# Dense weights unpacked one chunk further ahead, and token sums that begin later

## The chip, the cores and the metric

The kernel runs on one core of a Trainium2 chip. The metric is the device time of one execution in microseconds. The kernel before takes 569.09 us (median of three runs, 568.45 to 571.18).

## The reference

Three stages follow each other on the same 1536 tokens. Only the last one is touched by the change.

```python
attn_out = _attn_ref(q, k, v, n_sink, window)          # 2 x 8 heads, 768 positions, 64 wide; window of 128 and 4 sinks
x = attn_out.transpose(0, 2, 1, 3).reshape(1536, 512)
x = _moe_ref(x, w_gate, w1, w2)                        # 8 experts, 192 tokens each: relu(x @ w1[e]) @ w2[e]

def _moe2_ref(x, w_in, w_out):                         # the dense stage
    h = x @ w_in                                       # 512 -> 2048
    g = h * (1.0 / (1.0 + np.exp(-h)))                 # silu
    return (g @ w_out).astype(np.float32)              # 2048 -> 512
```

`w_in` and `w_out` are drawn as float64, so each of their numbers comes as two 32-bit words. The experts' weights are float32.

## The kernel before, in words

**Numbers in two halves.** A product is made from numbers split in a high and a low half (`float32r`): high by high, high by low, low by high, all added in one PSUM bank. So a chunk of weights goes through these steps before TensorE can use it: two or more loads of 512 KB on SP's queue (`raw`, lines 888 to 893); for the float64 ones the unpacking of the two words into a float32 tile `f64`, ten VectorE steps a half chunk (`s0` to `s4` twice, lines 912 to 932); and the split, a copy on ScalarE (`hi`, line 955) and a subtraction (`lo`, line 958) that is GpSimd's for float32 chunks and VectorE's for the late float64 ones.

**Chunks.** The class `Weights` numbers the chunks: 0 to 31 are the experts', 32 and 33 the first input and output chunk of the dense stage, then for each of three further parts of 512 hidden columns two input chunks and one output chunk: 34, 35, 36, then 37, 38, 39, then 40, 41, 42. The output chunks 36, 39 and 42 have two halves, each with a `hi` and a `lo`. The input chunks 34, 35, 37, 38, 40 and 41 go through `mix` (line 980) instead: besides two blocks as they are, four sums and differences of their blocks are made on GpSimd and split, ten GpSimd instructions a chunk (lines 1004, 1008 and 1015). `early` are 32 and 33, unpacked during the attention; `late` are 34 to 42.

**Two queues of steps.** `split(k)` is called when a buffer of the four `wr` buffers is given back (`done`). It puts the unpacking of chunk k in line (`ahead`, list `back`) and its split in line (list `todo`). In `dense`, after each turn, `W.pump(1, 1)` issues one step of `todo`, if its chunk is unpacked, and one step of `back`. The order of the engines' instructions is thus written out when the program is built: every engine runs its own in this order, and an instruction that must wait holds up all that is behind it on its engine.

**Passes of `dense`.** The loop over `n` (line 1466) makes 17 passes. Pass n computes the hidden columns of slot n (part c of four, token group g of two, half p of the part's columns), and the output products (`down`, line 1384) of slot n - 1. Passes 0 to 5 are plain: four products `u` of 12 matmuls (line 1271, 384 columns) and six `d` turns of 6 matmuls (line 1393, 512 columns), in the order `uuddduuddd`; pass 0 has no `d`. From pass 6 (`MIX`) on, seven `u` of 6 matmuls and six `d` take turns; a product over sums of tokens and sums of weights replaces one in four there, and some products are added into a tile `keep` on VectorE (line 1305), which frees the bank. The product banks `h` are two. ScalarE makes `Silu` (1257) and the high half of the result (1258), VectorE its low half (1450, `gt`). In the second and third part, six output tiles of a group are added to running sums, loaded from and stored to HBM (lines 1374, 1405 and 1409); this is in passes 6, 8, 10 and 12, and in the last part the sum goes out by rows.

**Token sums.** The mixed form needs sums and differences of the tokens. `mixing` (line 1319) gives them as lists of steps, 20 for each group (`made`), most of them one VectorE instruction (line 1426), six a copy on ScalarE (1329) and a subtraction on VectorE (1330), and eight more a group that overwrite x in its place (`placed`). The list `extra` holds them with the pass and turn from which each may be issued, and `also` issues one, or two in certain passes, behind each turn:

```python
extra = deque([(0, 0, f) for f in made[0][0] + made[1][0]] + ...)
def also(n, k):
    for _ in range(2 if n in (0, begin - 1) else 1): ...
```

Of the kernel before, what the change touches and what calls it, by code (L numbers as in the profile page):

```python
# [871 lines left out]
class Weights:  # L872
# [64 lines left out]
    def split(self):  # L937
        nc, k = self.nc, self.ns
        if k >= len(self.order):
            return  # L940
        self.ns += 1
        w = self.pool.tile([P, 2, CH], F32R, name="wr", bufs=self.depth)
        wide = k in self.wide
        self.ahead(k)
        if k in self.mixed:
            self.todo += [(0, f, (k, 0)) for f in self.mix(k, w, wide)]
            return
        for half in range(2):
            sl = slice(half * CH // 2, (half + 1) * CH // 2)

            def src(half=half):
                return self.box[k, half][0].bitcast(F32) if wide else self.raw[k][0]

            def hi(sl=sl, src=src):
                nc.scalar.activation(w[:, 0, sl], src(), AF.Copy)  # L955

            def lo(half=half, sl=sl, src=src):
                (nc.vector if k in self.late else nc.gpsimd).tensor_tensor(  # L958
                    w[:, 1, sl], src(), w[:, 0, sl].bitcast(F32), OP.subtract)
                self.used(k, half, w)  # L960
            self.todo += [(0, hi, (k, half)), (0, lo, (k, half))]

    def fresh(self):
        while self.full >= self.scratch:
            self.todo.popleft()[1]()
        self.full += 1
        return self.f64.tile([P, CH // 2], I32, name="f64", bufs=self.scratch)
# [132 lines left out]
def ffn(tc, rows, idx, ident, W, out, sums_d, mix_d):  # L1100
    with ExitStack() as ctx:
        x2 = ctx.enter_context(tc.tile_pool(name="f_x", bufs=1, side="right")).tile([P, 4, 2, B * S], F32R, name="x2")
        kk = [0]

        def nxt():
            kk[0] += 1
            return kk[0] - 1

        with rows.ctx, tc.tile_pool(name="e_p", bufs=1, space=PSUM) as pp:
            experts(tc, rows, lambda name: pp.tile([P, 2, 512], F32, name=name, bufs=2), ident, W, nxt, x2)  # L1110
        with tc.tile_pool(name="d_w", bufs=1, reuse_waits="tile") as gp, \
                tc.tile_pool(name="d_p", bufs=1, space=PSUM, reuse_waits="tile") as pp:
            dense(tc, gp, pp, idx, W, nxt(), x2, out, sums_d, mix_d)
# [123 lines left out]
def dense(tc, wp, pp, idx, W, first, x2, out, sums_d, mix_d):  # L1237
# [81 lines left out]
    def mixing(g):  # L1319
        t, q = keep[:2]  # L1320

        def at(j, s, b, d):
            return x2[:, 2 * j + d, b, tokens(g, s)].bitcast(F32)

        def tt(*a):
            return partial(nc.vector.tensor_tensor, *a)

        def split(dst, src, after=lambda: None):
            nc.scalar.activation(dst[0], src, AF.Copy)
            nc.vector.tensor_tensor(dst[1], src, dst[0].bitcast(F32), OP.subtract)  # L1330
            after()

        def keep_it():
            for n in range(3):
                nc.sync.dma_start(mix_d[g, :, n], xn[:, n].rearrange("p a d t -> p (a d t)").bitcast(F32))

        def new(n, d):
            return [xn[:, n, b, d] for b in range(2)]

        made, placed = [], []  # L1340
        for d in range(2):
            made += [
                tt(t, at(0, 1, 0, d), at(0, 0, 0, d), OP.subtract),
                tt(q, at(0, 1, 1, d), at(0, 0, 1, d), OP.subtract),
                tt(t, t, q, OP.add),
                partial(split, new(0, d), t),
                tt(q, at(1, 1, 0, d), t, OP.subtract),
                tt(q, q, at(1, 1, 1, d), OP.add),
                partial(split, new(1, d), q),
                tt(t, at(1, 0, 0, d), q, OP.subtract),  # L1350
                tt(t, t, at(1, 0, 1, d), OP.add),
                partial(split, new(2, d), t, keep_it if d else lambda: None),
            ]
            placed += [
                tt(t, at(1, 1, 0, d), at(0, 1, 0, d), OP.subtract),
                tt(q, at(1, 1, 1, d), at(0, 1, 1, d), OP.subtract),
                tt(t, t, q, OP.add),
                partial(split, [x2[:, d, b, tokens(g, 1)] for b in range(2)], t),
            ]
        return made, placed  # L1360
# [23 lines left out]
    def down(c, g, p, t, ahead):  # L1384
# [18 lines left out]
        def add():  # L1403
# [6 lines left out]
            if ahead is not None:  # L1410
# [3 lines left out]
    slots = [(c, g, p) for c in range(4) for g in range(2) for p in range(2)]  # L1414
    begin = slots.index(MIX)
    made = [mixing(g) for g in range(2)]
    extra = deque([(0, 0, f) for f in made[0][0] + made[1][0]] + [(4, 0, f) for f in made[1][1]] +
                  [(begin - 1, 2, f) for f in made[0][1]])

    def halves(n):  # L1420
        return (0, 1) if n < begin - 1 else (1, 0)

    def also(n, k):
        for _ in range(2 if n in (0, begin - 1) else 1):
            if extra and extra[0][:2] <= (n, k):
                extra.popleft()[2]()  # L1426

    for n in range(len(slots) + 1):
# [14 lines left out]
        for k, turn in enumerate(turns):  # L1443
            src = u if turn == "u" else down_at
            if not src:
                continue
            due = len(later)
            src.pop(0)()
            for _ in range(due):
                later.popleft()()  # L1450
            W.pump(1, 1 if n else 0)
            also(n, k)
# [223 lines left out]
```

## Time and profile before

| | |
|---|---|
| median of three runs | 569.09 us |
| profiled execution | 571.69 us, span 569.8 us |
| mean granted TensorE clock | 0.988 |
| TensorE busy | 546.6 us (96%) |
| VectorE busy | 354.9 us (62%) |
| ScalarE busy | 292.5 us (51%) |
| GpSimd busy | 287.0 us (50%) |
| DMA | 107.90 MB, mean 189 GB/s |

The span runs from the first to the last instruction, and the profiled execution's time is 1.89 us more. A busy share is a mean over stages with different limits; `dense` begins near 292 us and takes the rest. In `dense` TensorE is the engine that the others must keep up with, so what counts there is when it had to wait and what it waited for. In the rows further down, "idle" or a bracket before an arrow gives how long an engine stood before the instruction, and behind the arrow stands what released it. Matmul ends are modelled, so waits of TensorE are better read from the starts of its instructions.

### The profile page before, as it was taken

Reading aid. Unit: us, or ns where it says so; the run is one execution under the profiler, and the core shown is the slowest. Engines: PE = TensorE matmul, PEld = TensorE weight load, DVE = VectorE, ACT = ScalarE, POOL = GpSimd, SP = SyncE. Lnnn points to the kernel's source line nnn. Section 1 sums busy time; section 2 is a strip of 40 time slices with the busy share of each in tenths; the row PEclk is TensorE's granted clock in tenths of the full one; section 3 lists DMA queues with packets and bytes.
Section 4 is the critical chain, followed back from the end, with each engine's and each line's share of the span. In section 5 each row is a group of like instructions: output and inputs, shape, how many; then the busy total and the mean of one; then the engine's idle time right before and its main releaser. Section 6 shows DMA issues by size and latency. Waiting matters only on the chain.

```text
span 569.8 us, 9684 instructions
## 1 busy us (share of the span) xinstructions
PE 546.6 (96%) x3389; PEld 481.7 (85%) x3389; DVE 354.9 (62%) x923; ACT 292.5 (51%) x576; POOL 287.0 (50%) x278
## 2 busy tenths in 40 slices
PE   8999999878999999999999999998999999989996
PEld 4678677756999999999998899886997898979984
DVE  3788998773543443434358797875878657795423
ACT  4545554754676776777634563641454334544330
POOL 4334343296699999999990254200354006420404
PEclk9999999899999999999999999998999899999999
DMA  7998752144566666667640551623767647347602
GB/s 203 357 381 273 264 172 94 57 159 158 166 198 230 221 223 226 222 219 225 216 132 15 213 197 73 223 94 126 223 224 238 236 173 255 123 162 245 234 18 110
DMA packets 43934, 107.90 MB, mean 189 GB/s; under 512 B 4650, under 2 KB 12458, under 8 KB 43884
## 3 DMA queue, kind: packets, MB, share of 16 engines
q1 hardware_dynamic: 41696, 100.88, 52.7%
q0 software_dynamic: 1920, 6.29, 3.1%
q8 instruction: 27, 0.44, 0.3%
q14 instruction: 23, 0.19, 0.1%
q10 hardware_dynamic: 268, 0.10, 0.1%
HBM read 86.81 MB, written 20.45 MB: 188 GB/s over the span
## 4 chain that ended last, share of the span: by engine, by line
PE 59%; DVE 5%; issue 5%; DMA 2%; ACT 2%; POOL 2%; POOLq 0%; SPq 0%; DVEq 0%; another core or an unknown queue 0%; ACTq 0%
PE acc L1393 17%; PE h L1271 16%; PE mm L1178 8%; PE m L1201 8%; PE mm L1181 4%; PE m L1204 4%; DMA os<-sums_d 2%; POOL out L1364 2%; PE mm L1201 1%; DVE keep L1426 1%; DVE wr L958 1%; ACT wr L955 1%; PE mm L1137 1%; DVE os L1405 1%; DMA row<-x_d,idx 1%
## 5 line engine op out<-in xcount | busy, mean ns | idle before, releaser
L958 POOL TENSOR_TENSOR wr<-raw,wr 128x1024 fp32r<-128x1024 f32 x64 | 150.7, 2390 | 9.1 <-ACT wr L955 9.0
L1393 PE MATMUL acc<-wr,gt 128*128 128x512 f32 x576 | 148.6, 400 | 6.1 <-DVE wr L958 3.0
L1393 PEld LDWEIGHTS acc<-wr,gt 128*128 128x128 f32 x576 | 108.1, 190 | 28.1 <-DVE wr L958 4.3
L1271 PE MATMUL h<-x,wr 128*128 128x384 f32 x528 | 101.5, 338 | 1.8 <-ACT keep L1257 1.4
L1271 PEld LDWEIGHTS h<-x,wr 128*128 128x128 f32 x528 | 93.7, 188 | 6.2 <-ACT keep L1257 1.7
L1004 POOL TENSOR_TENSOR wr<-f,wr 128x512 fp32r<-128x512 f32 x12 | 16.7, 1394 | 127.6 <-ACT wr L999 67.4
L1178 PE MATMUL mm<-xg,wr 128*128 128x384 f32 x248 | 72.4, 360 | 0.5 <-DVE xg L1152 0.3
L955 ACT ACTIVATE wr<-raw 128x1024 fp32r<-128x1024 f32 x64 | 66.6, 1052 | 2.2 <-DMA raw<-in_w 1.3
L1201 PE MATMUL m<-ht,wr 128*128 128x384 f32 x224 | 66.0, 361 | 0.0
L1181 PE MATMUL mm<-xg,wr 128*128 128x192 f32 x248 | 62.1, 250 | 0.0
L1204 PE MATMUL m<-ht,wr 128*128 128x192 f32 x224 | 56.1, 250 | 0.0
L1450 DVE TENSOR_TENSOR gt<-keep,gt 128x384 fp32r<-128x384 f32 x64 | 38.4, 599 | 23.3 <-ACT gt L1258 23.2
L283 ACT ACTIVATE A<-t,nm 128x132 f32<-128x132 f32 x96 | 36.1, 400 | 30.9 <-DVE nm L274 30.7
L1178 PEld LDWEIGHTS mm<-xg,wr 128*128 128x128 f32 x248 | 46.4, 187 | 1.2 <-DVE xg L1152 0.7
L1181 PEld LDWEIGHTS mm<-xg,wr 128*128 128x128 f32 x248 | 47.2, 190 | 0.0
L1159 DVE TENSOR_TENSOR mm<-mm,t 128x384 f32<-128x384 f32 x33 | 18.7, 567 | 45.1 <-ACT t L1158 45.1
L305 POOL TENSOR_SCALAR_AFFINE_SELECT atd<-at 128x512 f32<-128x512 f32 x24 | 16.4, 685 | 59.2 <-ACT at L303 47.8
L1204 PEld LDWEIGHTS m<-ht,wr 128*128 128x128 f32 x224 | 42.7, 190 | 0.0
L1201 PEld LDWEIGHTS m<-ht,wr 128*128 128x128 f32 x224 | 42.0, 187 | 0.0
L1257 ACT ACTIVATE keep<-keep 128x384 f32<-128x384 f32 x30 | 15.8, 526 | 50.2 <-DVE keep L1305 50.2
L1298 ACT ACTIVATE keep<-h 128x384 f32<-128x384 f32 x30 | 14.7, 489 | 45.9 <-PE h L1271 42.0
L1271 PE MATMUL h<-xn,wr 128*128 128x384 f32 x180 | 38.2, 348 | 0.0
(197 smaller groups left out, 1012.9 us busy)
## 6 DMA issues: line engine op xcount, KB each, us to landing
raw<-in_w SPq DMA_DIRECT2D x64, 512.0 KB, 3.6
sums_d<-os SPq DMA_DIRECT2D x36, 256.0 KB, 2.1
xn<-mix_d SPq DMA_DIRECT2D x12, 768.0 KB, 5.2
raw<-in_wi SPq DMA_DIRECT2D x16, 512.0 KB, 4.4
raw<-in_wo SPq DMA_DIRECT2D x16, 512.0 KB, 4.3
os<-sums_d SPq DMA_DIRECT2D x24, 256.0 KB, 2.8
mix_d<-xn SPq DMA_DIRECT2D x6, 768.0 KB, 4.0
va<-in_va SPq DMA_DIRECT2D x12, 292.0 KB, 5.2
```

The source lines that it names most:

```text
L283: nc.scalar.activation(A[i][:, h], t, AF.Exp, bias=nm, scale=-1.0)
L955: nc.scalar.activation(w[:, 0, sl], src(), AF.Copy)
L958: (nc.vector if k in self.late else nc.gpsimd).tensor_tensor(w[:, 1, sl], src(), w[:, 0, sl].bitcast(F32), OP.subtract)
L1004: nc.gpsimd.tensor_tensor(w[:, 1, sl].rearrange("p (d f) -> p d f", d=4), src()[:, :, i * P:(i + 1) * P], w[:, 0, sl].bitcast(F32).rearran ...
L1159: nc.vector.tensor_tensor(h, h, t, OP.add)
L1178: nc.tensor.matmul(mm[:, b, :2 * CAP], w[:, 0, fb, d, o:o + P], x[:, d].rearrange("p a t -> p (a t)"), start=d == 0, stop=False, skip_grou ...
L1181: nc.tensor.matmul(mm[:, b, :CAP], w[:, 1, fb, d, o:o + P], x[:, d, 0], start=False, stop=d == 3, skip_group_check=True)
L1201: nc.tensor.matmul(mm[:, d % 2, :2 * CAP], w[:, 0, d // 2, f, o:o + P], ht[:, f].rearrange("p a t -> p (a t)"), start=c == 0 and f == 0, s ...
L1204: nc.tensor.matmul(mm[:, d % 2, :CAP], w[:, 1, d // 2, f, o:o + P], ht[:, f, 0], start=False, stop=last, skip_group_check=True)
L1271: nc.tensor.matmul(h, w(a, d), x(b, d), start=start and d == 0 and k == 0, stop=d == n - 1 and k == 2, skip_group_check=True)
L1393: nc.tensor.matmul(a, gt[:, u, ts], w[:, v, 2 * p + i], start=(p, i, k) == (0, 0, 0), stop=(p, i, k) == (1, 1, 2), skip_group_check=True)
L1450: later.popleft()()
```

## The change

It has three parts. `split(k)` also puts the unpacking of chunk k + 1 in line when both are late chunks. `fresh`, which issues steps of `todo` when all four `f64` tiles are taken, asserts that such a step is not still being unpacked; this adds no instruction. The first list of token sums begins at turn 2 of pass 0 instead of turn 0, that is with its third product, two steps a turn are issued in pass 1 alone (before: in passes 0 and 5), so that pass 0 has two of the steps (before: eight) and pass 1 twenty (before: ten).

```diff
--- before
+++ after
@@ -942,6 +942,8 @@
         w = self.pool.tile([P, 2, CH], F32R, name="wr", bufs=self.depth)
         wide = k in self.wide
         self.ahead(k)
+        if k in self.late and k + 1 in self.late:
+            self.ahead(k + 1)
         if k in self.mixed:
             self.todo += [(0, f, (k, 0)) for f in self.mix(k, w, wide)]
             return
@@ -962,6 +964,7 @@
 
     def fresh(self):
         while self.full >= self.scratch:
+            assert self.todo[0][2] not in self.unpacking
             self.todo.popleft()[1]()
         self.full += 1
         return self.f64.tile([P, CH // 2], I32, name="f64", bufs=self.scratch)
@@ -1414,14 +1417,14 @@
     slots = [(c, g, p) for c in range(4) for g in range(2) for p in range(2)]
     begin = slots.index(MIX)
     made = [mixing(g) for g in range(2)]
-    extra = deque([(0, 0, f) for f in made[0][0] + made[1][0]] + [(4, 0, f) for f in made[1][1]] +
+    extra = deque([(0, 2, f) for f in made[0][0] + made[1][0]] + [(4, 0, f) for f in made[1][1]] +
                   [(begin - 1, 2, f) for f in made[0][1]])
 
     def halves(n):
         return (0, 1) if n < begin - 1 else (1, 0)
 
     def also(n, k):
-        for _ in range(2 if n in (0, begin - 1) else 1):
+        for _ in range(2 if n == 1 else 1):
             if extra and extra[0][:2] <= (n, k):
                 extra.popleft()[2]()
 
```

The instructions of each engine stay the same in kind and number, TensorE's in order too. VectorE, ScalarE, GpSimd and SP get another order. Three places on VectorE follow; lines behind 943 are two or three higher after the change.

VectorE where `dense` begins, that is pass 0 and the first turns of pass 1, before (`keep_4671` and `keep_4672` hold token sums, `keep_4673` and `keep_4674` results of `Silu`, `x_2933` is x):

```order
L1426 TENSOR_TENSOR keep_4671<-x_2933 128x384
L1426 TENSOR_TENSOR keep_4672<-x_2933 128x384
L1450 TENSOR_TENSOR gt<-keep_4673,gt 128x384
L1426 TENSOR_TENSOR keep_4671<-keep_4671,keep_4672 128x384
L1330 TENSOR_TENSOR xn<-keep_4671,xn 128x384
L1450 TENSOR_TENSOR gt<-keep_4674,gt 128x384
L1426 TENSOR_TENSOR keep_4672<-x_2933,keep_4671 128x384
L1426 TENSOR_TENSOR keep_4672<-keep_4672,x_2933 128x384
L1450 TENSOR_TENSOR gt<-keep_4673,gt 128x384
```

and with the change:

```order
L1453 TENSOR_TENSOR gt<-keep_4673,gt 128x384
L1453 TENSOR_TENSOR gt<-keep_4674,gt 128x384
L1429 TENSOR_TENSOR keep_4671<-x_2933 128x384
L1453 TENSOR_TENSOR gt<-keep_4673,gt 128x384
L1429 TENSOR_TENSOR keep_4672<-x_2933 128x384
L1453 TENSOR_TENSOR gt<-keep_4674,gt 128x384
L914 TENSOR_SCALAR f_4762<-raw 128x512
L1429 TENSOR_TENSOR keep_4671<-keep_4671,keep_4672 128x384
L1333 TENSOR_TENSOR xn<-keep_4671,xn 128x384
L1453 TENSOR_TENSOR gt<-keep_4673,gt 128x384
```

The low halves `gt` of the first two products come first, then two subtractions for token sums, each behind a product; the first step with ScalarE (`xn`) comes behind the first unpacking step, which is pass 1's.

VectorE around the low half of the second half of chunk 36 (`f_5368` before, `f_5229` after), with the first running sum of pass 6 (`os`), before:

```order
L922 TENSOR_SCALAR f_5368<-f_5368 128x512
L926 SCALAR_TENSOR_TENSOR f_5368<-raw,f_5368 128x512
L930 SCALAR_TENSOR_TENSOR f_5368<-raw,f_5368 128x512
L914 TENSOR_SCALAR f_5502<-raw 128x512
L958 TENSOR_TENSOR wr<-f_5368,wr 128x1024
L918 TENSOR_SCALAR f_5502<-f_5502 128x512
L1405 TENSOR_TENSOR os<-acc,os 128x512
```

and with the change, where the first running sum of pass 6 comes 23 rows behind the low half:

```order
L930 SCALAR_TENSOR_TENSOR f_5229<-raw,f_5229 128x512
L914 TENSOR_SCALAR f_5385<-raw 128x512
L1453 TENSOR_TENSOR gt<-keep_4673,gt 128x384
L960 TENSOR_TENSOR wr<-f_5229,wr 128x1024
L918 TENSOR_SCALAR f_5385<-f_5385 128x512
L1453 TENSOR_TENSOR gt<-keep_4674,gt 128x384
L922 TENSOR_SCALAR f_5385<-f_5385 128x512
```

The low half stood among the first unpacking steps of pass 6 and now stands between two results of pass 5, with the unpacking of chunk 37 (`f_5385`) behind it.

VectorE in the second half of pass 8 (running sums `os`; additions into `keep`, line 1305 before and 1308 after; `f_5786` before and `f_5669` after are the first half of chunk 39, `f_5906` and `f_5779` its second half, `f_5890` chunk 40), before:

```order
L1450 TENSOR_TENSOR gt<-keep_4672,gt 128x384
L922 TENSOR_SCALAR f_5786<-f_5786 128x512
L1305 TENSOR_TENSOR keep_4673<-h,keep_4673 128x384
L1405 TENSOR_TENSOR os<-acc,os 128x512
L926 SCALAR_TENSOR_TENSOR f_5786<-raw,f_5786 128x512
L1450 TENSOR_TENSOR gt<-keep_4673,gt 128x384
L930 SCALAR_TENSOR_TENSOR f_5786<-raw,f_5786 128x512
L1305 TENSOR_TENSOR keep_4671<-h,keep_4671 128x384
L1405 TENSOR_TENSOR os<-acc,os 128x512
L914 TENSOR_SCALAR f_5906<-raw 128x512
L1450 TENSOR_TENSOR gt<-keep_4671,gt 128x384
L958 TENSOR_TENSOR wr<-f_5786,wr 128x1024
```

and with the change:

```order
L1308 TENSOR_TENSOR keep_4672<-h,keep_4672 128x384
L1408 TENSOR_TENSOR os<-acc,os 128x512
L930 SCALAR_TENSOR_TENSOR f_5779<-raw,f_5779 128x512
L1453 TENSOR_TENSOR gt<-keep_4672,gt 128x384
L914 TENSOR_SCALAR f_5890<-raw 128x512
L1308 TENSOR_TENSOR keep_4673<-h,keep_4673 128x384
L1408 TENSOR_TENSOR os<-acc,os 128x512
L960 TENSOR_TENSOR wr<-f_5779,wr 128x1024
L918 TENSOR_SCALAR f_5890<-f_5890 128x512
L1453 TENSOR_TENSOR gt<-keep_4673,gt 128x384
L922 TENSOR_SCALAR f_5890<-f_5890 128x512
L1308 TENSOR_TENSOR keep_4671<-h,keep_4671 128x384
L1408 TENSOR_TENSOR os<-acc,os 128x512
```

Before, the low half of chunk 39's first half stands last, behind the third addition into `keep`. Now that one stands ahead of the pass's first running sum, and the low half of the second half stands ahead of the third addition.

## Rows read from the trace of the kernel before

**Rows 1.** The page: busy time by engine, and TensorE's granted clock in 40 slices.

```profile
PE 546.6 (96%) x3389; PEld 481.7 (85%) x3389; DVE 354.9 (62%) x923; ACT 292.5 (51%) x576; POOL 287.0 (50%) x278
...
PEclk9999999899999999999999999998999899999999
```

**Rows 2.** Who TensorE waited for: us in total, times, longest.

```profile
PE acc L1393 <- DVE wr L958: 3.0, 4, 0.8
PE acc L1393 <- ACT wr L955: 3.0, 3, 1.5
PE h L1271 <- ACT keep L1257: 1.4, 1, 1.4
```

**Rows 3.** Timeline of TensorE, first products of passes: start, us, instruction, idle before.

```profile
301.65 4.49 PE L1271 MATMUL h<-x,wr 128*128 128x384 f32 x24 [1.36 <-ACT keep L1257]
...
318.59 4.39 PE L1271 MATMUL h<-x,wr 128*128 128x384 f32 x24
...
369.15 4.39 PE L1271 MATMUL h<-x,wr 128*128 128x384 f32 x24
...
387.27 1.22 PE L1271 MATMUL h<-x,wr 128*128 128x384 f32 x6
...
407.39 1.22 PE L1271 MATMUL h<-x,wr 128*128 128x384 f32 x6
...
423.14 1.22 PE L1271 MATMUL h<-x,wr 128*128 128x384 f32 x6
...
439.47 1.32 PE L1271 MATMUL h<-x,wr 128*128 128x384 f32 x6 [0.41 <-DVE keep L1305]
...
458.92 1.22 PE L1271 MATMUL h<-x,wr 128*128 128x384 f32 x6
...
474.67 1.31 PE L1271 MATMUL h<-x,wr 128*128 128x384 f32 x6
...
506.27 1.24 PE L1271 MATMUL h<-x,wr 128*128 128x384 f32 x6
...
524.09 1.22 PE L1271 MATMUL h<-x,wr 128*128 128x384 f32 x6
```

**Rows 4.** Stretches: PE, PEld, DVE, ACT, POOL busy (count), granted clock, DMA share, GB/s.

```profile
388.00:398.00 10.00, 7.71 (x29) 6.33 (x28) 4.54 (x8) 2.12 (x4) 0.00 (x0) 0.83 0.46 153
440.00:450.00 10.00, 8.49 (x33) 6.98 (x32) 7.06 (x14) 3.74 (x7) 0.00 (x0) 0.83 0.62 195
```

**Rows 5.** Timelines of GpSimd, VectorE and ScalarE around pass 0.

```profile
289.37 9.46 POOL L958 TENSOR_TENSOR wr<-f,wr 128x1024 fp32r<-128x1024 f32 x4
...
294.04 5.68 DVE L1426 TENSOR_TENSOR keep<-x 128x384 f32<-128x384 f32 x2
...
300.69 0.52 ACT L1329 ACTIVATE xn<-keep 128x384 fp32r<-128x384 f32 x1 [3.54 <-DVE keep L1426]
```

**Rows 6.** Timeline of VectorE, pass 8: a running sum, an unpacking step, an addition.

```profile
429.65 0.69 DVE L1405 TENSOR_TENSOR os<-acc,os 128x512 f32<-128x512 f32 x1 [1.32 <-DMA os<-sums_d]
430.26 0.42 DVE L922 TENSOR_SCALAR f<-f 128x512 int32<-128x512 int32 x1
...
438.87 0.55 DVE L1305 TENSOR_TENSOR keep<-h,keep 128x384 f32<-128x384 f32 x1
```

**Rows 7.** Unpacking: ten steps beside GpSimd (us, count), and a group alone (mean ns).

```profile
409.50:422.20 12.70, 8.96 (x10) 1.00 0.61 211
...
L926 DVE SCALAR_TENSOR_TENSOR f<-raw,f 128x512 int32<-128x512 int32 x2 | 1.4, 686 | 0.0
```

**Rows 8.** Timeline of VectorE: low halves of output chunks.

```profile
373.50 1.23 DVE L958 TENSOR_TENSOR wr<-f,wr 128x1024 fp32r<-128x1024 f32 x1 [0.39 <-ACT wr L955]
...
389.99 1.23 DVE L958 TENSOR_TENSOR wr<-f,wr 128x1024 fp32r<-128x1024 f32 x1 [2.96 <-ACT wr L955]
...
441.52 1.23 DVE L958 TENSOR_TENSOR wr<-f,wr 128x1024 fp32r<-128x1024 f32 x1 [0.39 <-ACT wr L955]
```

**Rows 9.** The page's costliest groups: GpSimd's blocks of mixed chunks.

```profile
L1004 POOL TENSOR_TENSOR wr<-f,wr 128x512 fp32r<-128x512 f32 x12 | 16.7, 1394 | 127.6 <-ACT wr L999 67.4
```

## The prediction

> **What bounds the kernel now.** I read the page first [rows 1]: TensorE is busy for 96% of the span, its granted clock is full but for three of the 40 slices, and VectorE (62%) and GpSimd (50%) have room over the whole. So only time in which TensorE waits, or runs at the lower clock, can be won. Second, who TensorE waited for [rows 2]: after the routing's sums, the largest entries are the two halves of a weight split, 3.0 us for VectorE's low half and 3.0 us for ScalarE's high half, and once 1.4 us for a `Silu`. All of these lie in `dense`, so third I read TensorE's timeline there at the first product of each pass [rows 3].
>
> That list of waits is too small, and the starts of the passes say by how much. A plain pass that meets nothing takes 16.85 us (three of them from 318.59 to 369.15), a mixed one 15.75 (pass 7, 407.39 to 423.14; pass 10, 458.92 to 474.67). Against these: pass 1 starts 1.36 late; pass 5 takes 18.12, 1.27 too long; pass 6 takes 20.12, 4.37 too long; pass 8 takes 16.33, 0.58 too long; pass 9 takes 19.45, 3.70 too long; passes 11 and 12 together 31.60, 0.10 too long; pass 13 takes 17.82, 2.07 too long. The sum is **13.45 us**, and it is the most this change can return. Part of it is the clock: two stretches of 10 us, behind the waits in passes 6 and 9, were granted 0.83 [rows 4], so TensorE ran there at 1.2 instead of 2.4 GHz for a while; at 0.17 of ten microseconds each fall cost 1.7 us. Passes 1, 5 and 13, late by 1.36, 1.27 and 2.07, show none: the page's digits for their slices are 9 [rows 1].
>
> **The change part by part.** *Token sums later.* In pass 0 ScalarE copies the first sum for the mixed form at 300.69, after 3.54 us of waiting for VectorE's subtractions, and the `Silu` that frees TensorE's product bank stands behind that copy in ScalarE's queue [rows 5]. VectorE was late since its first two subtractions took 5.68 us together while GpSimd ran four low halves of 2.37 us until 298.83. With the change no copy of a sum stands in ScalarE's queue in pass 0; the `Silu`s follow their products. VectorE's first instruction is then the low half of `gt`, as exposed to GpSimd as the subtraction was, and the third `Silu` overwrites what it reads. Even if it is held until 298.83 and takes another 0.55, it is done at 299.4, the `Silu` (0.5) at 299.9, and the bank is wanted at 300.3. **Gain 1.36.**
>
> The moved steps are not gone: pass 1 gets two sums a turn, 20, with ten unpack steps and four low halves of `gt`. At 0.55 (subtractions and sums, the shape of line 1305 in [rows 6]) and 0.53 (five unpack steps: three at 0.42 [rows 6] and two at 0.69 [rows 7]) that is 24 x 0.55 + 5.3 = 18.5 us in 16.85, some 2 us late, and as much again where VectorE waits for ScalarE's copies. What hides it: the next product on a bank starts half a plain pass, 8.4 us, after the last one there, which itself takes 2.1 (301.65 begins two, 24 matmuls in 4.2 net), so ScalarE may be some 6 us late. If that cover were gone, each microsecond beyond it would stall TensorE once. I take 0. The single instead of double steps in pass 5 end within that pass: 0.
>
> *Unpacking one chunk ahead.* No instruction is added. The ten unpack steps of a half, each with its load on SP's queue, stand one chunk earlier on VectorE; the copies and GpSimd's work on the input chunks follow, since they wait for the unpacking alone. Before, chunk 36's two halves end on VectorE at 373.50 + 1.23 and 389.99 + 1.23 and chunk 39's first at 441.52 + 1.23 [rows 8], inside the passes that are too long, and the list of waits names that line [rows 2]. With the change the low half of 36's second half stands ahead of the first running sum of pass 6, and the halves of 39 and 42 a pass before their use; that is half a pass ahead for 36's first half and a pass for the others. So the losses of pass 5 (1.27), pass 6 (4.37) and pass 13 (2.07) go, with the fall of the clock in pass 6, and in pass 9 all but the wait at its first product. The loads go ahead with the unpacking that frees their buffer, so each still has a pass or more before its words are read; SP's loads of running sums stand behind the same loads of `xn` as before.
>
> *What is late next: VectorE, at the ends of passes 6 and 8.* In passes 6, 8 and 10 it also adds six running sums (0.69 each, [rows 6]). In pass 8 the first can't run before its sum lands at 429.65 [rows 6]. From there to the third addition into `keep` before: four running sums, seven unpack steps, two low halves of `gt` and two additions, ending in an addition at 438.87, so that TensorE stood until 439.47, the 0.58 above. After: one unpack step more and the low half of weights (1.23) with them, 1.8 us more, but without GpSimd's work beside them, which had slowed them. Worked out alone: 4 x 0.69 + 8 x 0.53 + 4 x 0.55 + 1.23 = 10.4, less about 0.09 by which one of the 17 overlaps the next (line 1405 at 429.65 lasts 0.69, the next begins 0.61 after it), 9.0: the addition starts at 438.7 to 439.2. **I keep 0.7 lost there** (0.5 to 0.9). In pass 6 VectorE unpacks chunk 38 beside GpSimd's work on 37. The row for the same pair in pass 7 of before has ten steps at 8.96 us instead of 5.26 [rows 7]. With six running sums, three additions and four low halves of `gt` at some 0.6 and 0.47 net that is 8.96 + 3.6 + 3.3 = 15.9 in a pass of 15.75. The last addition must start 0.6 before the next pass does and would start up to 0.85 late by that row, or in time if GpSimd's last pieces miss it: **I take 0.4** (0 to 0.85). Pass 12 has no unpacking of a further chunk: 0, at most 0.7.
>
> The rule that speaks against such a pairing is the Trainium skill's, "SBUF — State Buffer", section "Who interferes with whom": a VectorE instruction with two SBUF inputs and a GpSimd one that reads SBUF hold a shared port in turn, and the one that comes second is blocked for the other's whole length. By it the first subtractions of rows 5 should each wait out about one low half, and 5.68 us for two agrees; in pass 7 the row's 0.37 us a step is less than one GpSimd instruction, so the sum goes by the row.
>
> Sum: 13.45 - 0.7 - 0.4 - 0.10 (pass 11, left as it is) = **12.2 us**. The profiled execution took 571.69 (span 569.8, 1.89 around it), which would become 559.5. It is 2.6 above the median of the runs, 569.09; taken off the median, **556.9**.
>
> **The rivals.** *VectorE's lateness takes the place of the weights' (0.23).* The additions stall at the ends of 6, 8 and 12 by the upper bounds, 0.85 + 0.9 + 0.7, and the clock falls twice as now: 13.45 - 2.45 - 3.4 = 7.6, so 561.5. For it: 15.9 of 15.75. Against it: pass 13's 2.07 brought no fall, and passes 6 and 7 have waits to give up.
>
> *The weights come late all the same (0.08).* If the words landed late, unpacking early would only move the wait from TensorE to VectorE, and the first part's 1.36 would be all: 567.7. Against it: no wait of VectorE for such a load stands in the trace; the DMA it waits for are the running sums.
>
> *GpSimd holds VectorE for its whole length (0.05), the slower side.* Ten GpSimd instructions a chunk at up to 1.39 [rows 9] would add 13.9 to the unpacking beside them: pass 6 comes to 5.3 + 13.9 + 6.9 = 26.1, 8.6 beyond the pass and the 1.8 us that an addition may be late; passes 7, 9 and 11 with 10 to 13 steps and no running sums to some 24, 6.5 each. That is 28 lost for 13.45 won, 584. It decides from about 16 us for ten steps, where pass 6 loses 5.5 and the other three 3.6 each, 16.3 for the 13.45. The row says 8.96. This is what the skill's rule above would do here if every step met GpSimd.
>
> **How the numbers follow.** The forecast has 0.64. Its own range is 555.3 (all 13.45 and a little noise) to 559.5 (each new wait at its upper bound, clock back); the first rival reaches 561.5, or 563 with passes 2 and 3 stalling as well. I give 555.2 to 563.0. Half a per cent is 2.8 us, about what a measurement of this kernel tells from no change: faster 0.87 (forecast and first rival), same 0.08 (the second), slower 0.05 (the third).
>
> **What would show it.** Right: ScalarE's copy of the first sum behind the `Silu` of pass 1 and no wait at pass 1's start; plain passes of 16.85 and mixed ones of 15.75 throughout, apart from the starts of 7 and 9; no wait of TensorE for a `wr`; 1.00 granted from 388 to 450. Wrong: a wait for `wr` or for `raw` left over, passes 2 and 3 longer than 16.85, the ten steps beside GpSimd above 9, or falls of the clock without waits.

## The result, and the profile after

The changed kernel takes 560.03 us (median of four runs, 559.35 to 561.95), the one before 570.13 beside it. The ratio is 0.9836, with a 95% interval of 0.9801 to 0.9871, so between 7.4 and 11.3 us were won. The forecast, 556.9, is 3.1 too low; the time lies inside the range of 555.2 to 563.0. The profiled execution of after is the slowest of its four runs: 561.95, span 560.0. Of all runs in this document one, 566.59 in experiment 8, was slow at a lower granted clock (0.98) and is left out.

On the page, beside [rows 1], TensorE is busy for 541.5 us instead of 546.6, and of the three slices with a lower clock one is left, the 32nd (the 8th lies ahead of `dense`, where the change touches nothing):

```profile
PE 541.5 (97%) x3389; PEld 479.7 (86%) x3389; DVE 353.0 (63%) x923; ACT 293.7 (52%) x576; POOL 292.8 (52%) x278
...
PEclk9999999999999999999999999999999899999999
```

TensorE's timeline at the first products of the passes, beside [rows 3] (start, length, instruction, idle before):

```profile
290.60 12.86 PE L1274 MATMUL h<-x,wr 128*128 128x384 f32 x72
...
315.92 4.39 PE L1274 MATMUL h<-x,wr 128*128 128x384 f32 x24
...
383.33 1.22 PE L1274 MATMUL h<-x,wr 128*128 128x384 f32 x6
...
399.08 1.22 PE L1274 MATMUL h<-x,wr 128*128 128x384 f32 x6
...
414.84 1.22 PE L1274 MATMUL h<-x,wr 128*128 128x384 f32 x6
...
427.75 1.32 PE L1274 MATMUL h<-x,wr 128*128 128x384 f32 x6 [0.50 <-DVE keep L1308]
...
433.90 1.89 PE L1274 MATMUL h<-x,wr 128*128 128x384 f32 x6 [2.01 <-DVE keep L1308]
...
451.32 1.25 PE L1274 MATMUL h<-x,wr 128*128 128x384 f32 x6
```

Passes 0 and 1 join without a wait (the row of 72 matmuls holds both first halves); passes 2 to 5 take 16.85 each (315.92 to 383.33), pass 6 15.75 (383.33 to 399.08), pass 7 15.76. Then pass 8 takes **19.06**, 3.31 too long, with two waits for additions into `keep`, and pass 9 takes **17.42**, 1.67 too long. The later passes take 15.75 to 15.79 each. That is 4.98 lost where 13.45 was lost before: 8.5 of the 9.8 by which the span is shorter. Another 1.05 lies ahead of `dense`, which begins at 290.60 instead of 291.65; that is not the change's, since in the runs below, all with the same program up to there, it begins anywhere from 289.5 to 292.7.

No wait for a `wr` is left. The low halves of chunk 36, beside [rows 8], on VectorE's timeline:

```profile
364.51 1.23 DVE L960 TENSOR_TENSOR wr<-f,wr 128x1024 fp32r<-128x1024 f32 x1 [0.39 <-ACT wr L957]
...
370.82 1.23 DVE L960 TENSOR_TENSOR wr<-f,wr 128x1024 fp32r<-128x1024 f32 x1 [0.39 <-ACT wr L957]
```

Both halves of 36 are there before pass 6 begins at 383.33. The granted clock, in stretches laid as in [rows 4]:

```profile
384.00:394.00 10.00, 10.00 (x51) 8.93 (x50) 6.30 (x12) 3.06 (x7) 6.61 (x6) 1.00 0.57 187
...
434.00:444.00 10.00, 10.00 (x43) 8.93 (x44) 6.47 (x13) 3.76 (x8) 1.18 (x1) 0.83 0.73 223
```

The stretch at the beginning of pass 6 has its full clock again; one fall is left, behind the waits at the end of pass 8.

Why pass 8 is late stands on VectorE's timeline there: the step that frees a buffer of words, the first and the third running sum, and the third addition into `keep`:

```profile
419.35 0.68 DVE L930 SCALAR_TENSOR_TENSOR f<-raw,f 128x512 int32<-128x512 int32 x1
424.08 0.69 DVE L1408 TENSOR_TENSOR os<-acc,os 128x512 f32<-128x512 f32 x1 [4.05 <-PE h L1274]
...
427.95 0.69 DVE L1408 TENSOR_TENSOR os<-acc,os 128x512 f32<-128x512 f32 x1 [0.25 <-DMA os<-sums_d]
...
433.30 0.55 DVE L1308 TENSOR_TENSOR keep<-h,keep 128x384 f32<-128x384 f32 x1
```

VectorE stood 4.05 us before the first running sum. (The release is put down to TensorE; but the first sum's load, issued at 415.41 below, took 8.6 us to land, until 424.0, and moving it takes the wait away, next section.) The sum came **9.24 us** into the pass, where 6.51 had been reckoned with. From it to the third addition it is 9.22. SP's queue around it:

```profile
413.32 0.33 SPq L892 DMA_DIRECT2D raw<-in_wo  x1
415.03 0.33 SPq L1305 DMA_DIRECT2D xn<-mix_d  x1
415.41 0.90 SPq L1377 DMA_DIRECT2D os<-sums_d  x2
420.06 0.33 SPq L892 DMA_DIRECT2D raw<-in_wo  x1
...
425.18 0.42 SPq L1377 DMA_DIRECT2D os<-sums_d  x1
```

The load of weights (`raw`) at 420.06 is the one that VectorE's step at 419.35 set free. It stands between the loads of the first two sums and that of the third; before the change it stood behind the fourth sum's:

```profile
432.40 0.43 SPq L1374 DMA_DIRECT2D os<-sums_d  x1
432.93 0.40 SPq L892 DMA_DIRECT2D raw<-in_wi  x1
```

### The profile page after: what moved, and what is told of

Read it like the earlier page. It is cut to its first block, busy times and chain, and to the rows that moved or that the text cites. A ratio compares the mean times of both kernels' runs of the same rounds, so it can differ in the third digit from the quotient of the medians.

```text
span 560.0 us, 9693 instructions
## 1 busy us (share of the span) xinstructions
PE 541.5 (97%) x3389; PEld 479.7 (86%) x3389; DVE 353.0 (63%) x923; ACT 293.7 (52%) x576; POOL 292.8 (52%) x278
## 4 chain that ended last, share of the span: by engine, by line
PE 66%; issue 4%; POOL 2%; DVE 1%; DMA 1%; ACT 0%; POOLq 0%; another core or an unknown queue 0%; DVEq 0%; ACTq 0%; SPq 0%
PE h L1274 20%; PE acc L1396 20%; PE mm L1181 9%; PE m L1204 8%; PE mm L1184 4%; PE m L1207 4%; POOL out L1367 2%; PE mm L1204 1%; PE mm L1140 1%; DMA row<-x_d,idx 1%; PE mm L1207 1%; DMA os<-sums_d 0%; DVE os L1408 0%; PE m L1181 0%; POOLq L1675 0%
## 5 line engine op out<-in xcount | busy, mean ns | idle before, releaser
L1396 PE MATMUL acc<-wr,gt 128*128 128x512 f32 x576 | 146.4, 397 | 0.0
L1007 POOL TENSOR_TENSOR wr<-f,wr 128x512 fp32r<-128x512 f32 x12 | 19.4, 1614 | 98.1 <-ACT wr L1002 98.1
L1453 DVE TENSOR_TENSOR gt<-keep,gt 128x384 fp32r<-128x384 f32 x64 | 42.0, 657 | 23.8 <-ACT gt L1261 23.8
L1367 POOL DMA_INDIRECT out<-raw,idx x12 | 11.6, 964 | 59.2 <-DVE raw L1408 59.0
L1274 PE MATMUL h<-xn,wr 128*128 128x384 f32 x180 | 36.9, 339 | 0.1
```

The lines of the kernel that those rows point to most:

```text
L1007: nc.gpsimd.tensor_tensor(w[:, 1, sl].rearrange("p (d f) -> p d f", d=4), src()[:, :, i * P:(i + 1) * P], w[:, 0, sl].bitcast(F32).rearran ...
L1274: nc.tensor.matmul(h, w(a, d), x(b, d), start=start and d == 0 and k == 0, stop=d == n - 1 and k == 2, skip_group_check=True)
L1367: i = nc.gpsimd.indirect_dma_start(out=out, out_offset=bass.IndirectOffsetOnAxis(ap=idx[:, t // 3, t % 3:t % 3 + 1], axis=0), in_=o, in_of ...
L1396: nc.tensor.matmul(a, gt[:, u, ts], w[:, v, 2 * p + i], start=(p, i, k) == (0, 0, 0), stop=(p, i, k) == (1, 1, 2), skip_group_check=True)
```

## The experiments

Eleven runs, each against the kernel before on the same chip. "Lost" is what a pass takes beyond 16.85 or 15.75 in the profiled execution.

**1. The sums' first loads early.**

```diff
+            if n < len(slots) and slots[n][2] == 1 and k == 8:
+                for t in [s * 3 + t for s in halves(n) for t in range(3)][:AHEAD]:
+                    bring(*slots[n][:2], t)
-            if slots[n - 1][2] == 1:
-                for t in ts[:AHEAD]:
-                    bring(*slots[n - 1][:2], t)
```

> The changed kernel, with the first two loads of running sums of passes 6, 8, 10 and 12 issued behind turn 8 of the pass before, instead of at the pass's own start. Theory (the sum lands late): in the changed kernel the first running sum of pass 8 began at 424.08, 9.24 us into the pass, where 6.51 had been reckoned with; the work of VectorE behind it took 9.22, as reckoned, and the pass's end came 3.31 late, with 1.67 more at the lower clock in pass 9. With the loads early VectorE doesn't wait there, passes 8 and 9 take 15.75 each, and the time falls by 4.98: 555.1. Rival (VectorE has too much to do in pass 8 wherever its sums come from): the third addition is at least 2 us late again and the clock falls again: 558 to 560.

Measured: 559.26, ratio 0.981 (0.978 to 0.984). The time is the rival's, the trace is neither's: the wait for the first sum is gone, and pass 8 still loses 1.49, pass 9 0.12. VectorE, pass 8 (415.51 to 432.75):

```profile
420.49 0.68 DVE L1408 TENSOR_TENSOR os<-acc,os 128x512 f32<-128x512 f32 x1
...
426.80 0.69 DVE L1408 TENSOR_TENSOR os<-acc,os 128x512 f32<-128x512 f32 x1 [2.04 <-DMA os<-sums_d]
```

It now stands 2.04 before the *third* sum. SP's queue shows why:

```profile
420.60 0.33 SPq L892 DMA_DIRECT2D raw<-in_wo  x1
...
421.57 0.42 SPq L1377 DMA_DIRECT2D os<-sums_d  x1
```

The load of weights, 512 KB, goes out at 420.60, the third sum's at 421.57, with only the store of the first sum between them; the sum lands 5.1 us later, and VectorE takes it up 5.2 us behind the issue. So a second late sum had been hidden behind the first.

**2. Two loads ahead of xn's only.** The same lines with `k == len(turns) - 2`.

> As the run with early loads, but the two loads stand right ahead of the last product of the pass before, that is behind the load of weights issued at 413.32 in the changed kernel and ahead of that of xn (768 KB) only. Theory (they wait behind the bytes of xn): the first sum lands about 3 us after its issue, well before 420.7, from which on each microsecond is lost: 555.1 like the early loads. Rival (the load of weights ahead or the one behind holds them): it lands after 420.7 and part of the 4.98 stays: 556 to 560.

Measured: 559.59, ratio 0.982 (0.9783 to 0.9858). VectorE, first and third sum:

```profile
420.64 0.68 DVE L1408 TENSOR_TENSOR os<-acc,os 128x512 f32<-128x512 f32 x1
...
427.04 0.69 DVE L1408 TENSOR_TENSOR os<-acc,os 128x512 f32<-128x512 f32 x1 [2.12 <-DMA os<-sums_d]
```

The first sum runs without a wait 4.97 us into the pass, so going ahead of xn's bytes is enough for it, and the load of weights ahead of both does not hold it. The third waits 2.12 as in the first experiment, and pass 8 loses 1.58.

**3. One part of the change alone.** Unpacking ahead without the later token sums:

```diff
-    extra = deque([(0, 2, f) ...
-        for _ in range(2 if n == 1 else 1):
+    extra = deque([(0, 0, f) ...
+        for _ in range(2 if n in (0, begin - 1) else 1):
```

> The unpacking one chunk ahead alone; the token sums as in the kernel before. Theory: the Silu behind the copy of the first sum makes pass 1 late again, 1.36, and nothing else differs from the changed kernel: 561.4. Rival (the doubled steps of pass 5 now collide with the unpacking of chunk 37 and the low halves of 36, which were moved into that pass): a wait in pass 5 or 6 as well, 562.5 or more.

Measured: 562.88, ratio 0.9886 (0.9849 to 0.9923): 1.5 above the number expected, which the one trace, of the fastest of the four runs (560.77), does not explain. TensorE at the starts of passes 1 and 9:

```profile
301.04 4.49 PE L1274 MATMUL h<-x,wr 128*128 128x384 f32 x24 [1.35 <-ACT keep L1260]
...
434.20 1.32 PE L1274 MATMUL h<-x,wr 128*128 128x384 f32 x6 [1.38 <-DVE keep L1308]
```

Pass 1 is late by what was expected, passes 5, 6 and 7 are right, and pass 8 loses 1.55. The rival falls by the trace. Here the first sum began 6.18 into pass 8 and the third waited 1.33.

Later token sums without the unpacking:

```diff
-        if k in self.late and k + 1 in self.late:
-            self.ahead(k + 1)
```

> The later token sums alone; the unpacking as in the kernel before. Theory: pass 1 starts in time and everything else stays, 570.13 - 1.36 = 568.8. Rival (the doubled steps of pass 5 had part in the late halves of chunk 36): pass 5's 1.27 goes too, and part of pass 6's 4.37: 567.5 down to 563.

Measured: 569.42 against 569.49, ratio 0.9988 (0.9961 to 1.0014). The trace has pass 1 in time; pass 5 loses its 1.27 as before, so the rival falls. A gain of 1.36 is 0.0024, inside the interval: this run can't show it in the time. Experiment 8 prices it again.

**4. Only the output chunks unpacked ahead.**

```diff
-        if k in self.late and k + 1 in self.late:
+        if k in self.late and k + 1 in self.late and k + 1 not in self.mixed:
```

> Of the unpacking ahead only what concerns the output chunks 36, 39 and 42: an input chunk is unpacked when it was before. Chunk 36 then stands where the change puts it; the first halves of 39 and 42 stay behind the third addition of passes 8 and 12, since input chunk 38 and 41 hold the line. Theory (each late half costs what it cost before): passes 5 and 6 are right, 15.75 in pass 6, while pass 9 keeps its waits for the halves of 39 (3.5 with the clock) and pass 13 its 2.07; against the changed kernel, which loses 1.5 to 5 in passes 8 and 9, 1 to 5 slower: 563. Rival (the lead of the input chunks is what counts): pass 6 is late again as well, 4 more: 567.

Measured: 566.27, ratio 0.9943 (0.992 to 0.9966). Between the two numbers, but the trace decides: pass 6 is right, and TensorE waits for the halves of 39 in pass 9 (and for those of 42 in pass 13), as it did before the change:

```profile
384.47 1.22 PE L1274 MATMUL h<-x,wr 128*128 128x384 f32 x6
...
400.23 1.22 PE L1274 MATMUL h<-x,wr 128*128 128x384 f32 x6
...
435.67 0.49 PE L1396 MATMUL acc<-wr,gt 128*128 128x512 f32 x1 [0.74 <-ACT wr L957]
436.93 2.28 PE L1396 MATMUL acc<-wr,gt 128*128 128x512 f32 x5 [0.77 <-DVE wr L960]
```

What the theory missed is pass 12, which loses 0.62, pass 13, which loses 3.70 instead of 2.07, and pass 8, which loses 1.87: its first sum was late here too, 7.84 into the pass (415.98), and the third addition came 9.18 behind it. VectorE at the first sum, and SP's queue ahead of it:

```profile
423.82 0.69 DVE L1408 TENSOR_TENSOR os<-acc,os 128x512 f32<-128x512 f32 x1 [1.70 <-DMA os<-sums_d]
```

```profile
414.33 0.33 SPq L892 DMA_DIRECT2D raw<-in_wi  x1
416.17 0.33 SPq L1305 DMA_DIRECT2D xn<-mix_d  x1
...
422.14 0.33 SPq L892 DMA_DIRECT2D raw<-in_wi  x1
```

So chunk 36's place is won by the output chunks' lead alone, and the places of 39 and 42 only if the input chunks go ahead as well.

**5. Four sums early.** As experiment 1, with

```diff
-MIX, AHEAD = (1, 1, 0), 2
+MIX, AHEAD = (1, 1, 0), 4
```

> As the first run with early loads, but four running sums instead of two are loaded ahead, all four behind turn 8 of the pass before. Theory (the third sum of pass 8 lands late, 5.2 us after its issue, since the load of weights that the unpacking frees stands right ahead of it on SP's queue; VectorE stood 2.04 for it, and the pass's end came 1.49 late): passes 8 and 9 take 15.75, and the time is 1.6 below that run's 559.26: 557.6. Rival (VectorE's work itself): pass 8 is at least 0.7 too long without any wait for a sum: 558.5 to 559.3.

Measured: **556.75** (555.86 to 559.22), ratio 0.9765 (0.9737 to 0.9792): faster than the changed kernel, too: four of the five runs lie below all ten of that kernel's, above and in experiment 10, of which the fastest took 558.37. TensorE at the first products of passes 8, 9 and 10:

```profile
416.95 1.22 PE L1274 MATMUL h<-x,wr 128*128 128x384 f32 x6
...
432.70 1.22 PE L1274 MATMUL h<-x,wr 128*128 128x384 f32 x6
...
448.46 1.25 PE L1274 MATMUL h<-x,wr 128*128 128x384 f32 x6
```

15.75 and 15.76, and no wait in `dense` at all. VectorE does the same work in pass 8, so the rival falls: it has the time, when its sums are there.

**6. Four sums ahead, at the pass's start.** `AHEAD` 4 in the changed kernel, nothing else.

> As the changed kernel, with four running sums instead of two loaded at the start of passes 6, 8, 10 and 12, so that the third is no longer behind the load of weights, but the first still behind that of xn. Theory: no wait for the third sum; the first at 6 to 9 us into pass 8, the chain behind it 9.2, so the pass ends 0 to 3 us late; 558 to 560. Rival (the third sum did not matter): pass 8 takes 17.3 again without a late first sum, 559.9.

Measured: 559.58, ratio 0.9822 (0.979 to 0.9853). VectorE, first sum and third addition (pass 8 begins at 413.96):

```profile
421.92 0.69 DVE L1408 TENSOR_TENSOR os<-acc,os 128x512 f32<-128x512 f32 x1 [2.90 <-DMA os<-sums_d]
...
430.83 0.55 DVE L1308 TENSOR_TENSOR keep<-h,keep 128x384 f32<-128x384 f32 x1
```

The third sum has no wait any more; the first, behind xn, came 7.96 into the pass, and 8.91 behind it the third addition. Pass 8 loses 1.73. So each of the two sums alone is enough to make it late.

**7. The load of weights behind the sums.** Loads of weights are counted instead of issued in turns 0 to 7 of the passes with running sums, and issued at turn 8.

```diff
+        if self.hold:
+            self.held += 1
+            return
...
+            if n and slots[n - 1][2] == 1 and 0 < slots[n - 1][0] < 3 and k in (0, 8):
+                W.hold = k == 0
+                while k and W.held:
+                    W.held -= 1
+                    W.load()
```

> As the changed kernel, with loads of weights held back in turns 0 to 7 of passes 6, 8, 10 and 12, so that in pass 8 the one stands behind the loads of the third and fourth sum; on the other engines nothing moves. Theory: the third sum lands some 2.7 us after its issue, pass 8 ends 0.2 late where it ended 1.5 late: 558.3. Rival (the sum is late for another reason, the stores of sums or xn): VectorE waits 1.3 to 2 us for it again and pass 8 takes 17.2: 559.9. If the held load is itself late for the unpacking, a later pass shows it.

Measured: 558.28, ratio 0.9809 (0.978 to 0.9838). VectorE, first sum, third sum and third addition; then TensorE at pass 9's first product:

```profile
420.30 0.69 DVE L1412 TENSOR_TENSOR os<-acc,os 128x512 f32<-128x512 f32 x1 [0.74 <-PE h L1278]
...
424.29 0.69 DVE L1412 TENSOR_TENSOR os<-acc,os 128x512 f32<-128x512 f32 x1 [0.38 <-DMA os<-sums_d]
...
429.64 0.55 DVE L1312 TENSOR_TENSOR keep<-h,keep 128x384 f32<-128x384 f32 x1
```

```profile
430.25 1.32 PE L1278 MATMUL h<-x,wr 128*128 128x384 f32 x6 [0.62 <-DVE keep L1312]
```

The third sum, issued at 421.38 with no load of weights ahead of it, is taken up 2.9 us later instead of 5.2, after a wait of 0.38 instead of 2.04. The first is there 6.58 into the pass, the third addition 9.34 behind it, and pass 8 loses 0.78, pass 9 0.11. That is more than the 0.2 expected, but without the late third sum. Only the order of SP's queue was edited, and the store of the first sum still stands ahead of the third's load (421.02), so the rival falls. The time itself can't tell 558.28 from 560.03.

**8. Four sums early, old token sums.** Experiment 5 with the first edit of experiment 3.

> The run with four running sums early, but with the token sums placed as in the kernel before, so that the part on token sums is priced where TensorE waits for nothing else in dense. Theory: pass 1 starts 1.36 late behind the Silu, and nothing else changes: 558.1 against 556.75. Rival (the lateness is made up, as the token sums alone were hardly faster: 569.42 against 569.49): 556.8.

Measured: 559.47 (557.32 to 559.95), ratio 0.9809 (0.9764 to 0.9854), against 556.75. TensorE at the start of pass 1:

```profile
301.34 0.97 PE L1274 MATMUL h<-x,wr 128*128 128x384 f32 x4 [1.35 <-ACT keep L1260]
```

The 1.35 is the only wait of TensorE in `dense`, and nothing makes it up; the rival falls. The medians differ by 2.7, more than the trace explains, from two sets of runs that overlap.

**9. Four sums early on the kernel before.**

> The kernel before with four running sums loaded early and nothing else changed. Theory (in the kernel before the sums cost TensorE only the late start of pass 9 and the 0.58 of pass 8; the loads of weights stood behind them): 569.5, at most 1 below the kernel before; the early sums pay only where the unpacking ahead has moved a load of weights in front of them. Rival (the early sums are worth 3 us by themselves): 566 or 567.

Measured: 570.15 against 570.13, ratio 0.9979 (0.995 to 1.0009). Pass 8 takes 15.95, pass 13 loses 1.77 instead of 2.07 and pass 11 nothing; the other losses are within 0.03 of those of before. Early sums win nothing that the time shows in the kernel before, where the first comes 6.51 into pass 8 and no load of weights stands between the second and the third.

**10. The changed kernel once more.**

> The changed kernel once more, as it is, beside the two others, for a second profile. Theory (the wait of 4.05 for the first sum of pass 8 and the fall of the clock behind it were that one execution's; the third sum's wait is in all): pass 8 takes 17.2 to 17.3, pass 9 15.9, and the time is 559.5 to 560. Rival (both belong to the changed kernel): passes 8 and 9 take 19 and 17.4 again, and the execution is near 562.

Measured: 559.63, ratio 0.9822 (0.9779 to 0.9866). VectorE's first sum in pass 8 (415.99 to 434.00), and the stretch that held the fall in the first profile:

```profile
424.26 0.69 DVE L1408 TENSOR_TENSOR os<-acc,os 128x512 f32<-128x512 f32 x1 [3.09 <-issue]
```

```profile
434.00:444.00 10.00, 9.99 (x49) 8.92 (x50) 7.48 (x15) 4.39 (x10) 1.29 (x1) 1.00 0.76 270
```

Between the theory and the rival: the first sum was late again, 8.27 into the pass, and pass 8 lost 2.26; the clock did not fall, and pass 9 lost 0.13. So the late first sum belongs to the changed kernel, and its size differs between executions; the fall was that one execution's.

## Why the prediction was right, and where it was not

**Token sums, 1.36: right.** Pass 1 starts in time in every run with the edit, 1.35 late in every run without it. How VectorE got there is as costed: its first two low halves in pass 0 lie beside GpSimd's work:

```profile
294.02 4.56 DVE L1453 TENSOR_TENSOR gt<-keep,gt 128x384 fp32r<-128x384 f32 x2 [0.95 <-ACT gt L1261]
```

4.56 us for two that take 0.56 alone (299.29 on the same timeline), done by 298.6 where 299.4 had been allowed. GpSimd's low halves there take 2.36 each (9.45 for four, 288.25 to 297.70). The Trainium skill, "SBUF — State Buffer", section "Who interferes with whom", lets the later of two such instructions wait for the other's whole length; this row, 2.28 for each of the two, agrees with it. The 20 steps of pass 1 stalled nothing: passes 1 to 5 are 16.85.

**Unpacking ahead, passes 5, 6 and 13 and part of 9: right.** 1.27, 4.37 and 2.07 are gone with every wait for `wr`, and experiment 4 shows them tied to the chunks that were named: where 39's and 42's halves stay late, passes 9 and 13 wait.

**Pass 6, 0.4: too high, nothing was lost.** The steps unpacked beside GpSimd, in passes 6 and 7:

```profile
383.30:399.00 15.70, 6.52 (x11) 1.00 0.68 217
401.70:413.60 11.90, 8.32 (x10) 1.00 0.65 225
```

Ten steps and the end of an eleventh take 6.52 in pass 6, and ten take 8.32 in pass 7, where 8.96 was taken for pass 6 [rows 7]. Four of pass 6's ten began behind 393.5, where GpSimd stands until 398.1. Nothing came near the 16 us from which the slower side decides.

**Pass 8, 0.7: the step that failed.** The chain was right: the third addition came 9.22 behind the first sum (9.0 forecast; 9.34 and 8.91 in experiments 7 and 6). What failed is the landing of the first sum at 6.51 into the pass, taken over from [rows 6] with the sentence that SP's loads of running sums stand behind the same loads of `xn` as before. That order holds for the first two sums (`xn` at 415.03, the sums at 415.41; 423.34 and 423.71 before), but they landed later behind it; and the third sum had a load of weights put ahead of it. Of the moved unpacking I had counted the steps and said of its loads that their own words are in time. I had not asked what they pass on SP's queue. In the changed kernel's two profiles the first sum came at 9.24 and 8.27, and the pass lost 3.31 and 2.26; the 1.67 at the lower clock behind the first of these stands in the sum at nothing. With all four sums ahead of the load of weights and of xn (experiment 5) the pass lost nothing.

The third sum's part is shown by experiments 1 and 7. For the first, experiments 1 and 2 show that it is in time with its load ahead of xn's. Why it is late behind xn's is open. The load of weights behind it can't be the whole reason: in experiment 4 that load went out 6.16 into the pass and the first sum came at 7.84, in the unpacking ahead alone it went out sooner, 5.86, and the sum came at 6.18. What goes with the lateness in these profiles is the load of weights ahead of xn's: it went out 1.7 to 1.9 us before that one where the first sum came at 7.8 to 9.2 (the changed kernel twice, experiments 4 and 6), and 1.1 to 1.2 before it where the sum came at 6.2 to 6.6 (the kernel before, each part of the change alone, experiment 7). In the third microsecond of the pass, when none of these loads of weights behind the sums was out, the core's DMA moved 129 GB/s in the changed kernel and 135 in experiment 4, against 375 in the kernel before. No run moves that load by itself, and experiment 7, with 6.58 and 0.78 lost, moved both.

**The sum.** Forecast: 13.45 won, less 0.7, 0.4 and 0.1. Measured in the profile: less 3.31 and 1.67; in the second one, less 2.26 and 0.13. Between the medians 10.1 was won, where 12.2 was forecast. The time lies in the range that was given, but above the forecast's own, which ended at 559.5, and nearer to the first rival's 561.5 than to 556.9. That 559.5 does not come out of its terms: the upper bounds, 0.85, 0.9, 0.7 and 0.1, leave 10.9, which is 558.2. And losses read from an execution 2.6 above the median were taken off the median, though some 1.5 of them is not lost in every execution (last section).

**The rivals.** The first, VectorE's lateness in place of the weights', came true at one of its three places, pass 8, by a late load and not by VectorE's work; passes 6 and 12 were right. The second falls with the halves of [rows 8], the third with the 6.52 and 8.32.

## What to carry to other kernels

When work moves ahead, follow the loads that it sets free as far as the work itself: ask on the issuing queue which small, urgent loads each large one now stands in front of. A load that is waited for early in a stretch belongs in the stretch before, ahead of the large ones, as many as there are buffers; here four early loads won some 3 us more, while the same edit won nothing in the kernel before. And when a wait is gone but the time stays, look for the next wait on the same engine: the third sum was late behind the first.

## What was unexpected

The fall of the clock does not follow from the waits alone. In the token sums' run TensorE met in pass 6 the same two waits as the kernel before in its (1.52 and 0.77, at 390.01 and 391.27 there):

```profile
387.47 0.49 PE L1394 MATMUL acc<-wr,gt 128*128 128x512 f32 x1 [1.52 <-ACT wr L955]
388.73 1.45 PE L1394 MATMUL acc<-wr,gt 128*128 128x512 f32 x5 [0.77 <-DVE wr L958]
```

Yet the first of these two stretches of that run, laid to pass 6 as the first of [rows 4], kept its clock; the second, with the waits of pass 9, did not:

```profile
385.50:395.50 10.00, 7.71 (x37) 6.30 (x36) 5.19 (x9) 2.42 (x4) 0.00 (x0) 1.00 0.60 194
435.00:445.00 10.00, 8.10 (x31) 6.71 (x32) 7.97 (x15) 3.77 (x7) 0.00 (x0) 0.83 0.57 178
```

Pass 6 took 18.58 there instead of 20.12, 1.54 less, about what had been put down to the fall. So some 1.5 of the 13.45 is not lost in every execution with the old order of unpacking. The changed kernel's two profiles differ the same way: behind a wait of 2.01 at pass 9's first product the stretch had 0.83, behind one of 2.02 it had 1.00.

The load of a running sum, 256 KB, took from 2.6 to 8.8 us from issue to landing in one execution of the changed kernel.
